# Attention and MLP in one core: more elementwise work for GpSimd, a planner that counts eight transfers, and free PSUM banks for the last layer

## The chip, the cores and the metric

The kernel runs on one core of a Trainium2 chip. The metric is the device time of one execution in microseconds (us), the median of several runs. A core has TensorE (PE, matrix multiply, written to PSUM), VectorE (DVE), ScalarE (ACT) and GpSimd (POOL) for elementwise work, and SyncE (SP), which here issues all DMA transfers. Each engine runs its own instructions in order; they wait for each other through semaphores. In the profile, PEld is the loading of weights into PE.

## The reference

Attention where a query sees only the keys of its own hash bucket, over 4 batches, 8 heads, 768 positions and 64 dimensions, and then an MLP on the 3072 resulting rows:

```python
q_bucket = np.sum((np.einsum('bhsd,dk->bhsk', q, proj) > 0) * powers, axis=-1)   # 6 bits; k likewise
mask = q_bucket[:, :, :, None] == k_bucket[:, :, None, :]
scores = np.where(mask, scale * np.matmul(q, k.transpose(0, 1, 3, 2)), -1000000000.0)
attn = softmax(scores)
x = np.matmul(attn, v)             # laid out as 3072 rows of 512
h = np.maximum(x @ w_in, 0.0)      # w_in 512 x 2048
out = (h * h) @ w_out              # w_out 2048 x 512
```

## The kernel before, in words

Float32 products are made from pairs of half-precision numbers: each operand is split into a high part and the difference that the high part leaves, and three products (high by high, high by low, low by high) are summed in PSUM. Splitting is a copy (`move`, lines 465 to 471) and a subtraction (`left`, lines 473 to 477; for the weights the lines 579 and 580 in `split`). Much of the elementwise work is this.

**Attention** goes in units of 128 queries of one head (`unit`, line 739), 192 in all, six to a visit: one visit is a pair of heads and half of the positions (384 rows). A unit's scores are gathered by four matmuls in `pS`, two PSUM banks (for some early ones `pS2`, in the banks of `po`); DVE moves them out to `e` and takes the extreme value; ACT takes the exponential; the reciprocal of the sum, `rv`, is made on GpSimd or DVE; then `hl`, the high part (ACT) and the difference (DVE, since its scale is a vector), and a transposing DMA into `aT`. In the first four visits (`PLAIN_AV`) GpSimd multiplies `e` by `rv` instead and PE transposes it (`pT`), out of which ACT moves it to `aT`. `av` (line 783) multiplies with the values into `pA`, one bank, and leaves `xx`, again in two parts. `prep` (line 631) makes ready what a head needs: `A` and `L` are the two parts of the input `R`, `M` and `Q` carry the mask of the buckets, moved about by small DMAs. `first` (line 664) does it for the first visit with fewer steps, and uses `codes`.

**The MLP** (`moe`, line 807) has eight layers of 384 rows (a batch and a half each), and may run as soon as the four visits of its rows are done. Of its 16 steps f, each takes twelve `pm` matmuls, then relu (`g32`), the square (`square`, line 561), the high part `g[:, 0]` and the difference `g[:, 1]`; and a step later nine `po` matmuls, three for each of three groups t of 128 rows. The tile `po` has three banks, one for each group. After the last step the three groups are moved out to `o` and sent. There is one `pm` and one `po`, and two buffers of `g` and `g32`. The weights are fetched and split (`fetch`, `split`) during the first visits and the first layer, and `verify` reads all inputs again and checks that they lie in the range for which this fast way holds; the second half of the last layer's steps waits for its answer.

**The order** is made by a planner at build time. The code above doesn't issue instructions; it adds operations to a `Program`, some with several possible engines ("ways"). `add` (line 169) works out dependencies from the regions that operations touch (`region`, line 156); `order` simulates all five queues forward and backward several times and keeps the shortest plan; `emit` issues the instructions of each queue in the order of the plan. So whatever the planner believes of the chip sets which engine an operation gets and its place in the queue; the waits themselves are made afterwards, by the tile framework. Its beliefs are:

- `cost` (line 195): nanoseconds of each operation.
- `PRICE` (line 42): in the choice of an engine (lines 365 to 372) the operation's time is multiplied by it, and what else is ready for that engine is added.
- `port` (line 235): which operations hold something that DVE and GpSimd share; `forward` does not start one while another holds it (lines 361 to 363, 374 to 376).
- `region`: for PSUM, the banks an access touches, where two reads of one bank are ordered too (line 184).
- the transfers: how long SP is taken by issuing one, and when it lands (lines 384 to 391).

`LOW_BY` (line 63) names the engines that may take the differences of the weight splits.

## Time and profile before

| | |
|---|---|
| median of three runs | 832.88 us (832.54 to 834.76) |
| the profiled execution | 834.86 us, its span 833.1 us |
| granted TensorE clock, mean over the span | 0.994 |
| bytes moved by DMA | 145.93 MB, of which 56.80 MB read from HBM and 6.29 MB written |
| instructions | 14383 |

The span runs from the first to the last instruction; the time of the execution also holds what lies around it. All comparisons of busy time, idle time and waits are against the span. In a view of the profile, a row such as "PE x <- ACT y: 5.7, 8, 0.9" says that PE stood idle for 5.7 us in all, 8 times, 0.9 us at the longest, in front of an operation that writes x, until ACT's operation on y ended. A row of the timeline gives the start, the length, the engine, the line, the operation, out<-in with partitions x elements, how often it ran in a row, and in square brackets the idle time before it with what ended it. Nearly all operations have line 427, where the planner's helper issues them, so they are told apart by tile and shape.

### The profile page before, as it was taken

To read this page: it belongs to the slowest core of one execution; us is meant where nothing else is said; L and a number is where in the kernel's file an instruction comes from. 1 tells how busy PE (TensorE), PEld (TensorE's weight loads), DVE (VectorE), ACT (ScalarE), POOL (GpSimd) and SP (SyncE) were. 2 spreads that over 40 slices of the span, in tenths; PEclk is the share of its full clock that TensorE was granted. 3 is DMA by queue.
4 is the path that set the end of the run, shared out by engine and by line. 5 is a ranking of instruction groups with operands and counts; after the bars stand their busy time and mean duration, and the time that the engine had idled before them with its cause. 6 is when DMAs were issued, how large, how long until landed. Compare 5 with 4: busy or idle time off the path is not lost. (4 is left out here: it accounts for less than half of the span.)

```text
span 833.1 us, 14383 instructions
## 1 busy us (share of the span) xinstructions
PE 794.3 (95%) x5001; PEld 430.0 (52%) x5001; DVE 605.2 (73%) x1200; ACT 656.6 (79%) x1238; POOL 72.7 (9%) x175
## 2 busy tenths in 40 slices
PE   7797799999999999999999999999999999999996
PEld 4354355555555554555555545555555554555553
DVE  6888989998999888898879755888889433611110
ACT  5898999998888989888898856888988997334443
POOL 1255200100000010000000000000002000000000
PEclk9999999999999999999999999999999999999999
DMA  8985979999999999999989866988975889501001
GB/s 258 270 223 181 292 188 179 214 176 195 183 202 196 195 188 213 192 181 219 194 188 186 212 165 140 181 143 148 146 133 99 239 290 304 212 1 39 1 1 42
DMA packets 299521, 145.93 MB, mean 175 GB/s; under 512 B 268752, under 2 KB 279344, under 8 KB 299440
## 3 DMA queue, kind: packets, MB, share of 16 engines
q1 hardware_dynamic: 299440, 144.93, 77.2%
q8 instruction: 41, 0.67, 0.3%
q14 instruction: 40, 0.33, 0.1%
HBM read 56.80 MB, written 6.29 MB: 76 GB/s over the span
## 5 line engine op out<-in xcount | busy, mean ns | idle before, releaser
L427 PE MATMUL po<-wo,g 128*128 128x512 f16 x1152 | 296.9, 379 | 5.7 <-ACT o L427 5.7
L427 PE MATMUL pm<-xx,win 128*128 128x384 f16 x1536 | 297.7, 326 | 4.4 <-ACT g L427 2.8
L427 PEld LDWEIGHTS <-win 128*128 128x128 f16 x1536 | 149.9, 98 | 116.6 <-issue 8.0
L427 DVE TENSOR_SCALAR_CACHE_REDUCE e<-pS 128x768 f32<-128x768 f32 x192 | 182.7, 953 | 21.9 <-PE pS L427 17.7
L427 ACT ACTIVATE e<-e,maxes 128x768 f32<-128x768 f32 x192 | 178.2, 929 | 20.7 <-DVE e L427 19.2
L427 DVE SCALAR_TENSOR_TENSOR hl<-e,rv,hl 128x768 f16<-128x768 f32 x168 | 171.0, 1019 | 18.8 <-ACT hl L427 17.8
L427 PEld LDWEIGHTS <-g 128*128 128x128 f16 x1152 | 111.9, 98 | 124.8 <-issue 9.1
L427 ACT ACTIVATE hl<-e,rv 128x768 f16<-128x768 f32 x168 | 154.6, 923 | 6.0 <-DMA aT<-hl 5.2
L427 DVE SCALAR_TENSOR_TENSOR g<-g,g 128x384 f16<-128x384 f32 x121 | 66.9, 553 | 111.8 <-ACT g L427 111.4
L427 ACT ACTIVATE g<-g 128x384 f32<-128x384 f32 (+1 forms) x251 | 129.4, 517 | 6.6 <-PE po L427 2.7
L427 ACT ACTIVATE g<-pm 128x384 f32<-128x384 f32 x127 | 61.2, 482 | 90.3 <-PE pm L427 90.0
L427 PE MATMUL pS<-A,Q 128*128 128x384 f16 x372 | 93.1, 330 | 4.1 <-DVE e L427 2.6
L427 PE MATMUL pS<-L,M 128*128 128x384 f16 x372 | 91.8, 327 | 0.8 <-DMA M<-Q 0.8
L424 PE MATMUL pA<-aT,VV 128*64 128x384 f16 x1008 | 87.2, 327 | 0.0
L427 POOL TENSOR_SCALAR rv<-sums 128x1 f32<-128x1 f32 x136 | 36.8, 271 | 541.7 <-ACT e L427 400.2
L424 PEld LDWEIGHTS <-VV 128*64 128x64 f16 x1008 | 54.7, 110 | 32.9 <-issue 10.0
L427 PEld LDWEIGHTS <-Q 128*128 128x128 f16 x372 | 34.2, 98 | 43.1 <-issue 16.2
L427 DVE TENSOR_SCALAR M<-pc,masks 128x384 f16<-128x384 f32 x64 | 43.0, 672 | 15.4 <-PE pc L427 15.2
L427 PEld LDWEIGHTS <-M 128*128 128x128 f16 x372 | 36.3, 98 | 25.1 <-DMA M<-Q 1.2
L427 ACT ACTIVATION_READ_ACCUMULATOR e<-e,maxes 128x1 f32 x192 | 36.6, 191 | 0.0
L427 DVE SCALAR_TENSOR_TENSOR L<-R,A 128x768 f16<-128x768 f32 x32 | 30.4, 950 | 7.7 <-ACT A L427 7.5
L427 PE MATMUL pT<-unit_f,e 128*128 128x128 f32 x144 | 23.8, 293 | 10.5 <-ACT aT L427 7.7
(82 smaller groups left out, 517.4 us busy)
## 6 DMA issues: line engine op xcount, KB each, us to landing
R<-kq SPq DMA_DIRECT2D x32, 384.0 KB, 3.8
X<-kq SPq DMA_DIRECT2D x32, 384.0 KB, 4.1
raw<-w_in SPq DMA_DIRECT2D x16, 511.8 KB, 5.6
raw<-w_out SPq DMA_DIRECT2D x16, 511.8 KB, 4.9
V<-vp SPq DMA_DIRECT2D x20, 384.0 KB, 5.1
out<-o SPq DMA_DIRECT2D x24, 256.0 KB, 2.7
X<-vp SPq DMA_DIRECT2D x16, 384.0 KB, 4.4
Q<-L SPq DMA_DIRECT2D x32, 96.0 KB, 2.9
```

The lines of the kernel that those rows point to most:

```text
L424: ins = q.engine.matmul(*map(real, args), **kw).ins
L427: ins = getattr(q.engine, o.name)(*map(real, o.args), **{k: real(x) for k, x in o.kw.items()}).ins
```

## The change

The planner gets other beliefs, and the MLP other PSUM tiles at its end:

- `PRICE`: ACT 0.3 becomes 1, GpSimd 3.06 becomes 1.5.
- `port`: a DVE operation with two tensor inputs in SBUF no longer counts as a holder of what is shared with GpSimd; only copies and `tensor_scalar` do.
- `region`: an access to a PSUM tile counts as one to the whole tile, and two reads of it are no longer ordered.
- `cost`: pairs of matmuls with 64 rows of weights are counted as partly beside each other.
- `LANES`: the planner holds SP back where eight transfers are under way.
- `codes` shares its buffer with `g32`.
- in the last layer the three groups are gathered in the two banks of `pS` and the bank of `pA`, which attention no longer needs, instead of in `po`.
- the move of group t = 1 out of PSUM goes to DVE; that of the others may still go to ACT or DVE.

```diff
-PRICE = dict(pe=1, dve=3.57, act=0.3, pool=3.06, sp=0.43)
+PRICE = dict(pe=1, dve=3.57, act=1, pool=1.5, sp=0.43)
...
+LANES = 8
...
         if rec.kind == "psum":
-            return 0, 1, f0 // 512, 1 + (f0 % rec.row + size(ap.ap[1:]) - 1) // 512, 0, 0, 0
+            return 0, 1, 0, 1, 0, 0, 0
...
-                if (w or w2 or rec.kind == "psum") and a0 < p1 and p0 < a1 and b0 < f1 and f0 < b1 and not (fs and fs == bs and (c1 <= g0 or g1 <= c0)):
+                if (w or w2) and a0 < p1 and p0 < a1 and b0 < f1 and f0 < b1 and not (fs and fs == bs and (c1 <= g0 or g1 <= c0)):
...
             t = sum(size(a[2]) * column.get(a[2].dtype, 1 / 2.4) + 7 for a, _ in args) / side
+            if args[0][0][1].shape[0] == D and len(args) == 2:
+                t *= 0.5 if args[0][0][2].dtype == F32 else 0.7
             return t, t
...
-        return inside and (len(ins) == 2 or name in ("tensor_copy", "tensor_scalar"))
+        return inside and name in ("tensor_copy", "tensor_scalar")
...
                 dma += done
                 done = dma + 910 - t
+                if k != "pool":
+                    lanes.append(t + done)
+                    if len(lanes) >= LANES:
+                        busy = max(busy, lanes[-LANES] + 60 - t)
...
-        codes = sb([P, 4 * P], BF16, "codes")
+        codes = sb([P, 4 * P], BF16, "codes", 2, tag="g32")
...
                 if first:
-                    po = ps([P, 3, DM], F32, "po")
+                    if fast and n == 2 * B - 1:
+                        po = ps([P, 2, 512], F32, "pS"), ps([P, 512], F32, "pA")
+                        po = [po[0][:, 0], po[0][:, 1], po[1]]
+                    else:
+                        po = ps([P, 3, DM], F32, "po")
+                        po = [po[:, t] for t in range(3)]
...
                     elif last:
                         o = sb([P, DM], F32, "o", tag="f")
-                        move(o, po[:, t], back)
+                        move(o, po[t], back, (dve,) if fast and t == 1 else (act, dve, pool))
                         send(out[r0 : r0 + P], o)
```

More of the change, by code (lines that the diff above doesn't have):

```diff
@@ L326, in forward @@
         free = dict.fromkeys(keys, 0.0)
-        out, dma, dge, held, kind = [], 0.0, 0.0, 0.0, None
+        out, dma, dge, held, kind, lanes = [], 0.0, 0.0, 0.0, None, []
         def offer(i):
@@ L848, in moe @@
                     pr.rank, pr.mark = RANK_PE, pace()
-                    pe.matmul(po[:, t], gh, wo[:, 0, m], start=first, stop=False)
-                    pe.matmul(po[:, t], gh, wo[:, 1, m], start=False, stop=False)
-                    pe.matmul(po[:, t], gl, wo[:, 0, m], start=False, stop=last)
+                    pe.matmul(po[t], gh, wo[:, 0, m], start=first, stop=False)
+                    pe.matmul(po[t], gh, wo[:, 1, m], start=False, stop=False)
+                    pe.matmul(po[t], gl, wo[:, 0, m], start=False, stop=last)
                     pr.mark = None
@@ L861, in moe @@
                         if m == 3:
-                            move(acc[:, t], po[:, t], back)
+                            move(acc[:, t], po[t], back)
                         else:
-                            dve.scalar_tensor_tensor(acc[:, t], po[:, t], back, acc[:, t], ALU.mult, ALU.add)
+                            dve.scalar_tensor_tensor(acc[:, t], po[t], back, acc[:, t], ALU.mult, ALU.add)
                         if m == NF - 1:
```

## The prediction, made before the changed kernel was run

> **What bounds the kernel now.** I read the page's first two parts first: the busy shares and the 40 slices.
>
> ```profile
> span 833.1 us, 14383 instructions
> PE 794.3 (95%) x5001; PEld 430.0 (52%) x5001; DVE 605.2 (73%) x1200; ACT 656.6 (79%) x1238; POOL 72.7 (9%) x175
> PE   7797799999999999999999999999999999999996
> ...
> DVE  6888989998999888898879755888889433611110
> ACT  5898999998888989888898856888988997334443
> ...
> PEclk9999999999999999999999999999999999999999
> ```
>
> TensorE (PE) is nearly full from slice 6 on, at a granted clock of 0.9 or more throughout. Its idle time is 833.1 - 794.3 = 38.8 us, and only that can be won. The view of busy time by stretch says where it lies:
>
> ```profile
> 0.00:104.00 104.00, 80.78 (x523) 46.38 (x524) 85.51 (x189) 86.63 (x173) 36.56 (x54) 0.97 0.83 245
> 104.00:650.00 546.00, 540.50 (x3523) 293.46 (x3522) 470.95 (x925) 471.35 (x859) 36.18 (x121) 1.00 0.90 179
> 650.00:720.00 70.00, 68.10 (x399) 35.55 (x398) 28.65 (x52) 54.14 (x122) 0.00 (x0) 1.00 0.91 286
> 720.00:833.00 113.00, 104.93 (x562) 54.60 (x560) 20.07 (x37) 44.46 (x87) 0.00 (x0) 0.98 0.07 26
> ```
>
> After length come busy PE, PEld, DVE, ACT, POOL. PE idles 23.2 us in the front (first attention units, no MLP work yet), 5.5 us in the long middle, 1.9 and 8.1 us later. So off-loading DVE and ACT in the middle wins at most 5.5 us: there PE, not they, sets the time. After 720 us DVE and ACT are mostly idle already. The waits of PE name what it lacked:
>
> ```profile
> PE pT L427 <- ACT aT L427: 7.7, 8, 2.2
> PE po L427 <- ACT o L427: 5.7, 8, 0.9
> PE pc L427 <- ACT bits L427: 3.0, 2, 2.8
> ...
> PE pT L427 <- POOL e L427: 2.5, 3, 1.1
> ...
> PE pS L427 <- DMA A<-A: 1.3, 1, 1.3
> PE pS L427 <- DMA M<-Q: 0.8, 1, 0.8
> ```
>
> The second row is what the change can reach most surely. The timeline of the end shows its form:
>
> ```profile
> 822.75 1.46 PE L427 MATMUL po<-wo,g 128*128 128x512 f16 x6
> ...
> 824.25 0.60 ACT L427 ACTIVATE o<-po 128x512 f32<-128x512 f32 x1 [1.64 <-PE po L427]
> ...
> 824.90 0.81 PE L427 MATMUL po<-wo,g 128*128 128x512 f16 x3 [0.69 <-ACT o L427]
> ...
> 825.74 0.60 ACT L427 ACTIVATE o<-po 128x512 f32<-128x512 f32 x1 [0.90 <-PE po L427]
> 826.39 0.59 PE L427 MATMUL po<-wo,g 128*128 128x512 f16 x2 [0.69 <-ACT o L427]
> ```
>
> The three matmul groups of one `po` tile lie in three banks, yet the second waits until the first has been moved out, and the third for the second: 0.69 us each. The wait is on the tile, not on the bank, while the planner's `region` of before counts banks and so puts the move ahead of the next group.
>
> **The change part by part.** First a piece of the chain of waits, for a length that is needed at once:
>
> ```profile
> 752.32 1.95 PE pm L427 x12
> ```
>
> *The whole PSUM tile as one region, the DVE move for t=1, free banks for the last layer.* With whole tiles, a move depends on all groups written before it in program order, so the three groups run together and then the three moves. The 8 stalls, 5.7 us, go; what is late next is the following layer's first `po` group, which must wait for the moves: about 2 x 0.60 on ACT beside one on DVE. Twelve `pm` matmuls, 1.95 us, lie between and cover it; without that cover it costs 7 handovers x 1.2 = 8.4 us. The last layer doesn't wait even then, its banks (`pS`, `pA`) being free. Bounds -5.7 and +2.7 (8.4 - 5.7); I take **-5**, near the rows that show the stalls. Eight moves of t=1 go to DVE, behind whatever DVE runs at that moment; that is hidden by the same `pm`. The read-against-read orders that go away concern only moves on two engines; no row of PE's waits names one, so 0.
>
> *GpSimd's share.* I read "a third" as a third of 192 differences (128 `g`, 32 `L`, 32 weight splits) and of 144 squares. The prices:
>
> ```profile
> L427 POOL TENSOR_SCALAR e<-e,rv 128x768 f32<-128x768 f32 x24 | 24.5, 1028 | 14.9 <-PE pT L427 6.1 <-DVE rv L427 5.9 <-ACT aT L427 2.2
> L427 POOL TENSOR_TENSOR g<-g,g 128x384 f16<-128x384 f32 x7 | 6.5, 933 | 15.1 <-ACT g L427 9.8 <-DVE rv L427 3.1 <-issue 2.1
> L427 POOL TENSOR_TENSOR win<-f,win 128x512 f16<-128x512 f32 x3 | 3.5, 1173 | 4.1 <-ACT win L427 4.0
> ```
>
> ```profile
> L427 DVE SCALAR_TENSOR_TENSOR hl<-e,rv,hl 128x768 f16<-128x768 f32 x166 | 168.9, 1019 | 18.7 <-ACT hl L427 17.8
> ...
> L427 DVE SCALAR_TENSOR_TENSOR g<-g,g 128x384 f16<-128x384 f32 x79 | 43.4, 550 | 6.3 <-ACT g L427 6.0
> ...
> L427 DVE SCALAR_TENSOR_TENSOR L<-R,A 128x768 f16<-128x768 f32 x24 | 22.8, 951 | 3.6 <-ACT A L427 3.4
> ```
>
> ```profile
> L427 ACT ACTIVATE g<-g 128x384 f32<-128x384 f32 x86 | 44.4, 517 | 1.1
> ```
>
> The DVE rows and the ACT row are those of the middle alone. A GpSimd square and a GpSimd `L` aren't in the trace. The square lies between DVE's 0.55 and 1.17 (more columns); I take 0.93, the same two-input form. `L` lies between 1.03 (one input) and 1.87 (twice 0.93); I take 1.87. In the middle about 20 more `g` differences, 30 squares, 8 `L` and 3 splits move: 20 x 0.93 + 30 x 0.93 + 8 x 1.87 + 3 x 1.17 = 65 us onto GpSimd. DVE loses 20 x 0.55 + 8 x 0.95 + 3 x 0.68 (split, 0.68 in the timeline below) = 20.6 us, ACT 30 x 0.517 = 15.5 us. As PE is full, none of it counts directly.
>
> What counts is what the moved work does to DVE. Two places in the trace show a GpSimd operation beside a DVE operation with two SBUF inputs:
>
> ```profile
> 639.80 0.92 POOL L427 TENSOR_TENSOR g<-g,g 128x384 f16<-128x384 f32 x1 [2.70 <-ACT g L427]
> 639.83 1.71 DVE L427 SCALAR_TENSOR_TENSOR hl<-e,rv,hl 128x768 f16<-128x768 f32 x1
> ...
> 647.06 1.00 DVE L427 SCALAR_TENSOR_TENSOR hl<-e,rv,hl 128x768 f16<-128x768 f32 x1
> ```
>
> ```profile
> 19.12 0.69 DVE L427 TENSOR_TENSOR win<-f,win 128x512 f16<-128x512 f32 x1
> ...
> 80.00 2.73 POOL L427 TENSOR_SCALAR e<-e,rv 128x768 f32<-128x768 f32 x2
> 80.04 1.92 DVE L427 TENSOR_TENSOR win<-f,win 128x512 f16<-128x512 f32 x2 [0.34 <-ACT win L427]
> ...
> 82.89 0.48 PE L427 MATMUL pS<-A,Q 128*128 128x384 f16 x2 [1.39 <-DVE e L427]
> ```
>
> `hl` took 1.71 instead of 1.00 us; two splits took 1.92 instead of 2 x 0.69, two `e` 2.73 instead of 2.06, and PE then stood 1.39 us for DVE. So each meeting costs about 0.71 us, and the new `port` tells the planner that it costs nothing. In the middle, `hl`, `g` and `L` alone are 168.9 + 43.4 + 22.8 = 235 of 546 us of DVE, 43%; 61 moved operations x 0.43 x 0.71 = 18.6 us of blocking, about what DVE was relieved of. DVE therefore stays near 471 of 546 us, with some 75 us of slack, but the slack is no longer where the plan has it. Between none and all reaches PE: 0 and +18.6. I take **+2**, one in ten, since the seven `g` on GpSimd today stand in a middle with 5.5 us of PE idle time in all.
>
> The Trainium skill, page "SBUF — State Buffer", section "SBUF: two separate sides", says that GpSimd and a DVE operation with two SBUF inputs lock a shared port for whole instructions, the later one blocking fully. By that, the 0.89 us of overlap at 639.83 would cost 0.89 (the trace has 0.71) and the blocking 61 x 0.43 x 0.89 = 23.3 us; it speaks against the new `port`.
>
> *The front.* It begins and ends with these:
>
> ```profile
> 6.78 1.55 PE L424 MATMUL pS<-K,G 64*128 64x384 f32 x4
> ...
> 97.70 0.32 PE L427 MATMUL pm<-xx,win 128*128 128x384 f16 x1 [1.04 <-ACT xx L427]
> ```
>
> About 3 `L` and 4 splits leave DVE: 3 x 0.95 + 4 x 0.69 = 5.6 us of 85.5; meetings give back 7 x 0.43 x 0.71 = 2.1. ACT, as busy (86.6), gets relief where the price 1 in place of 0.3 sends copies elsewhere. GpSimd has 104 - 36.6 = 67 us free, but its `e` (24 x 1.03) sit on each unit's path to `pT`, and a 1.17 or 1.87 us piece ahead of one delays it. Bounds: the front's idle time without the 6.8 us until the first data matmul, 23.2 - 6.8 = -16.4, and +7.2 (four units each behind a 1.8 us piece). I take **-2**, about half of what DVE sheds.
>
> *Eight transfers under way.* Nothing on the chip changes by it but SP's order. The stalls it counts exist in the front:
>
> ```profile
> SPq L427 <- DMA raw<-w_out: 6.6, 6, 1.7
> SPq L427 <- DMA L<-M: 6.0, 3, 4.6
> ```
>
> PE itself waited for transfers only 1.3 + 0.8 = 2.1 us (rows above), so it is worth -2.1 to +2.1; I take 0. The factor for 64-row matmuls concerns the first visit's scores, `codes` in a `g32` buffer is read long before `g32` is written: 0.
>
> **Sum:** -5 + 2 - 2 = -5 us. The profiled execution took 834.86 us (span 833.1, 1.8 around it); it becomes 829.9. The median of before, 832.88, is 2.0 lower, so the forecast is **827.9**.
>
> **The rivals.**
>
> *GpSimd blocks DVE on the path (slower).* The place is the middle: DVE's `e` out of `pS` comes late, and PE, in order, stands as at 82.89. On top of 18.6 us of blocked DVE, a GpSimd square or difference that starts behind `hl` waits for half of 1.02, 61 x 0.43 x 0.51 = 13.4 us, on the way to `po`. For it: the rows above, and a planner blind to it. Against: DVE's 75 us of slack, MLP matmuls that fill PE. It decides once 7 + 2.5 = 9.5 of these 32 us, 30%, reach PE. At 60%: -7 + 19 = +12, **845**. By the skill's lock, with 0.89, it is +15. Chance 0.26.
>
> *Nothing comes of it.* The handover stalls become waits for the moves (ACT is 86% busy in the middle, so a move queues), front and blocking cancel: -1, **832**. Chance 0.17.
>
> *The front opens.* ACT and DVE both shed a tenth of the front's 86 us, and the MLP starts 8 us earlier: -5 + 2 - 8 = -11, **822**. For it: GpSimd idle there. Against: PE waits there mostly for ACT's `aT` and `bits`, which GpSimd can't take. Chance 0.13.
>
> *The planner keeps GpSimd idle*, because ready queues on ACT and DVE stay short: only the handovers, -5, with no blocking, **828**, as forecast. Chance 0.05.
>
> **How the numbers follow.** The forecast has 0.39. This kernel's measurement can tell about 0.3%, 2.5 us, from no change. Faster: 0.35 of the forecast's 0.39, the front's 0.13, the idle GpSimd's 0.05 and 0.02 of "nothing comes of it": 0.55. Same: the forecast's other 0.04 and 0.14 of "nothing": 0.18. Slower: 0.26 and the last 0.01: 0.27. The terms' bounds span -24 to +31 us; cutting 0.1 at each end gives 816 to 845. The forecast's own range is 823 to 831.
>
> **What would show it.** Right: no `po` wait on `o`; the last two moves on two engines; GpSimd near 150 to 200 us busy; DVE's busy time about as before, with `hl` above 1.02 us; PE idle in the middle still near 5 us. Wrong: PE waits on DVE `e` or GpSimd `g` above 10 us in the middle (the blocking), `po` waits that stay, or a first `pm` well before or after 97.7 us (the front). The first falls if GpSimd's `g` is much longer than 0.93 us.

## The result, and the profile after

The changed kernel takes **845.26 us** (median of four runs, 842.59 to 848.99); the kernel before, beside it, 833.63 (832.54 to 834.76). The ratio is 1.0154, its 95% interval 1.0118 to 1.0189. The forecast was 827.9 with a range of 816 to 845: a change forecast to win 5 us costs 11.6, and the time lies just above the range. The profiled execution took 846.62 us, 11.8 more than that of before.

First the page of the changed kernel, the busy shares and the slices:

```profile
span 844.8 us, 14501 instructions
PE 805.8 (95%) x5014; PEld 436.0 (52%) x5014; DVE 548.5 (65%) x1053; ACT 615.3 (73%) x1143; POOL 338.3 (40%) x417
PE   8787779999999999999999999999999999999996
...
DVE  4788779878888788878888603787889241045000
ACT  3788888897888878888888755777786468763342
POOL 2699875344243543333344332343222222331221
PEclk9899899999999999999999999999999999999999
```

The relief came: DVE is 57 us less busy (605.2 to 548.5), ACT 41 (656.6 to 615.3). But GpSimd (POOL) went from 72.7 to 338.3 us, not to the 150 to 200 of the prediction, and it is nearly full in slices 3 to 5, where the row of before has the digits 5, 5 and 2:

```profile
POOL 1255200100000010000000000000002000000000
```

PE stands idle as long as before, 844.8 - 805.8 = 39.0 us against 38.8, and is 11.5 us busier with the same arithmetic. So the idle time of PE, on which the prediction was built, doesn't show the loss. One reason is in the last row: in slices 2 and 5 the granted clock is below 0.9, and a slow matmul counts as busy.

The view of busy time by stretch, with the stretches of before (after length: PE, PEld, DVE, ACT, POOL, granted clock), has all of it in the first row:

```profile
0.00:104.00 104.00, 81.37 (x471) 47.40 (x472) 76.38 (x163) 76.76 (x148) 75.26 (x80) 0.90 0.82 246
...
104.00:650.00 546.00, 538.03 (x3488) 291.09 (x3487) 429.31 (x812) 430.71 (x775) 214.74 (x280) 1.00 0.88 174
...
650.00:720.00 70.00, 68.78 (x410) 36.13 (x408) 22.17 (x50) 47.77 (x96) 16.74 (x19) 1.00 0.60 145
...
720.00:844.00 124.00, 117.64 (x651) 61.41 (x648) 20.67 (x30) 60.10 (x126) 31.59 (x39) 0.99 0.37 123
```

In the first 104 us PE is as busy as before (81.37 against 80.78) but runs 471 matmuls instead of 523, at a granted clock of 0.90 instead of 0.97.

To have one number for this I worked out PE's **lost time**: each matmul is given the spacing that its form has in an unbroken run at full clock (`pm` and scores 0.163 us, `po` 0.216, and so on; the `idle` matmuls that only fill gaps, zero), and the lost time at t is t minus the spacings of all matmuls begun by then. The arithmetic is 776.1 us in both kernels. Lost time, in us:

| by | 20 | 60 | 97 | 130 | 650 | last matmul |
|---|---|---|---|---|---|---|
| before | 12.8 | 22.2 | 33.8 | 36.1 | 45.4 | 50.5 |
| after | 15.6 | 30.8 | 42.0 | 52.3 | 59.3 | 61.1 |

By 130 us the changed kernel has lost 52.3 - 36.1 = **16.2 us more**; from there to the end it loses 8.8 instead of 14.4, **5.6 less**. The last matmul begins 10.7 us later, and the end comes another 1 us later. Such a count is of the one profiled execution of a kernel, while its time is a median; the two lie up to 3 us apart (here 846.62 and 845.26, before 834.86 and 832.88).

The loss belongs to the front, the gain to the handovers. One more of PE's waits before, beside those that the prediction shows:

```profile
PE pS L427 <- DVE e L427: 2.6, 4, 1.4
```

And after:

```profile
PE pT L434 <- POOL e L434: 8.2, 7, 2.3
PE pS L434 <- DVE e L434: 6.9, 14, 1.2
...
PE pT L434 <- ACT aT L434: 2.9, 4, 2.0
...
PE po L434 <- POOL g L434: 1.5, 3, 0.8
...
PE po L434 <- ACT o L434: 0.6, 1, 0.6
```

These waits of PE show both. `po` on `o` fell from 5.7 to 0.6 us. `pT` on GpSimd's `e`, which exists only in the first four visits, rose from 2.5 to 8.2, and `pS` on DVE's `e` from 2.6 to 6.9. But `pT` on ACT's `aT` fell from 7.7 to 2.9, so the waits also moved from ACT to GpSimd and DVE: in the first 130 us PE's idle time grew by 4.4 us in all (23.8 to 28.2), about a quarter of the 16.2.

What GpSimd does in the front is in the groups of the first 98 us. Before, DVE alone:

```profile
L427 DVE SCALAR_TENSOR_TENSOR f<-raw,top 128x512 uint32<-128x512 uint32 x22 | 15.3, 698 | 0.9 <-ACT top L427 0.9
...
L427 DVE TENSOR_TENSOR win<-f,win 128x512 f16<-128x512 f32 x10 | 7.8, 785 | 1.5 <-ACT win L427 1.5
L427 DVE SCALAR_TENSOR_TENSOR L<-R,A 128x768 f16<-128x768 f32 x8 | 7.6, 950 | 4.1 <-ACT A L427 4.1
L427 DVE TENSOR_TENSOR wo<-f,wo 128x512 f16<-128x512 f32 x7 | 4.8, 679 | 0.0
```

After, GpSimd:

```profile
L434 POOL TENSOR_SCALAR e<-e,rv 128x768 f32<-128x768 f32 x22 | 26.7, 1222 | 5.1 <-DVE rv L434 5.0
L434 POOL TENSOR_TENSOR win<-f,win 128x512 f16<-128x512 f32 x10 | 12.3, 1233 | 12.1 <-ACT win L434 11.8
L434 POOL TENSOR_TENSOR L<-R,A 128x768 f16<-128x768 f32 x6 | 9.9, 1645 | 0.0
L434 POOL TENSOR_TENSOR wo<-f,wo 128x512 f16<-128x512 f32 x6 | 7.9, 1312 | 2.1 <-ACT wo L434 1.8
L434 POOL TENSOR_SCALAR win<-f 128x512 f16<-128x512 f32 x6 | 4.4, 735 | 2.9 <-DVE f L434 2.6
...
L434 POOL TENSOR_SCALAR wo<-f 128x512 f16<-128x512 f32 x5 | 3.8, 756 | 0.9 <-DVE f L434 0.6
```

And DVE:

```profile
L434 DVE SCALAR_TENSOR_TENSOR f<-raw,top 128x512 uint32<-128x512 uint32 x22 | 20.7, 939 | 3.2 <-ACT top L434 3.2
...
L434 DVE TENSOR_TENSOR win<-f,win 128x512 f16<-128x512 f32 x4 | 4.6, 1157 | 1.6 <-POOL win L434 1.3 <-ACT win L434 0.3
L434 DVE SCALAR_TENSOR_TENSOR L<-R,A 128x768 f16<-128x768 f32 x2 | 3.5, 1746 | 1.2 <-ACT A L434 1.2
...
L434 DVE TENSOR_TENSOR wo<-f,wo 128x512 f16<-128x512 f32 x2 | 1.5, 750 | 0.5 <-POOL wo L434 0.5
```

GpSimd took 6 of 8 `L`, 16 of the weights' differences and 11 of their high parts. What stayed on DVE grew longer each time: `f`, the same 22 operations, from 698 to 939 ns, `L` from 950 to 1746, `win` from 785 to 1157. Worse, GpSimd's `e` stands in one queue with all this. Two timelines show one case of each mechanism; first the collision:

```profile
18.23 1.65 POOL L434 TENSOR_TENSOR L<-R,A 128x768 f16<-128x768 f32 x1
18.30 2.12 DVE L434 TENSOR_TENSOR win<-f,win 128x512 f16<-128x512 f32 x1 [0.74 <-POOL win L434]
...
20.35 0.94 DVE L434 TENSOR_SCALAR_CACHE_REDUCE e<-pS 128x768 f32<-128x768 f32 x1
...
21.35 0.91 PE L431 MATMUL pS<-K,G 64*128 64x384 f32 x2 [1.07 <-DVE e L434]
```

A difference that takes 0.69 us alone took 2.12 behind GpSimd's `L`; DVE's move of the scores came late, and PE stood 1.07 us. Then the queue, in GpSimd's own timeline:

```profile
46.36 2.22 POOL L434 TENSOR_SCALAR e<-e,rv 128x768 f32<-128x768 f32 x2 [0.32 <-DVE rv L434]
48.55 1.65 POOL L434 TENSOR_TENSOR L<-R,A 128x768 f16<-128x768 f32 x1
50.16 1.60 POOL L434 TENSOR_TENSOR win<-f,win 128x512 f16<-128x512 f32 x1
51.85 0.19 POOL L434 TENSOR_SCALAR rv<-sums 128x1 f32<-128x1 f32 x1
52.13 0.62 POOL L434 TENSOR_SCALAR win<-f 128x512 f16<-128x512 f32 x1
52.83 1.47 POOL L434 TENSOR_TENSOR win<-f,win 128x512 f16<-128x512 f32 x1
54.29 0.90 POOL L434 TENSOR_SCALAR e<-e,rv 128x768 f32<-128x768 f32 x1
```

Between one unit's `e` and the next there are 5.7 us of other work almost without a gap. In the timeline of all engines the second `e` could have begun at 52.57 us, when DVE had made its reciprocal; it waited 1.7 us behind the two pieces of `win`, and PE's `pT` 0.39 us for it. The first `pm`, which waits for the `xx` at the end of the first attention, came at 112.26 instead of 97.70 us:

```profile
112.26 0.32 PE L434 MATMUL pm<-xx,win 128*128 128x384 f16 x1 [0.23 <-ACT xx L434]
```

At the other end, the kernel's last matmuls and moves:

```profile
836.60 0.60 ACT L434 ACTIVATE o<-pS 128x512 f32<-128x512 f32 x1 [2.22 <-PE pS L434]
837.23 2.04 SPq L434 DMA_DIRECT2D out<-o  x3
837.23 0.69 DVE L434 TENSOR_SCALAR o<-pS 128x512 f32<-128x512 f32 x1 [58.51 <-ACT o L434]
837.68 0.60 ACT L434 ACTIVATE o<-pA 128x512 f32<-128x512 f32 x1 [0.48 <-PE pA L434]
```

The groups no longer wait for the moves. But DVE's move, of another bank of the same tile, began only when ACT's had ended, and the row names ACT's `o` as what it waited for. The stretch from the last matmul's end to the span's end grew from 833.1 - 826.98 = 6.1 to 844.8 - 837.64 = 7.2 us. The transfers, now issued in a row, explain little of that: the last one was issued at 838.93 and landed 2.9 us later, 4.2 us after the last matmul; before, it was issued at 827.64 and landed 3.3 us later, 4.0 us after it. What fills the rest isn't known.

### The profile page after: what moved, and what is told of

It is laid out like the page before. It is cut to its first block, busy times and chain, and to the rows that moved or that the text cites. A ratio compares the mean times of both kernels' runs of the same rounds, so it can differ in the third digit from the quotient of the medians.

```text
span 844.8 us, 14501 instructions
## 1 busy us (share of the span) xinstructions
PE 805.8 (95%) x5014; PEld 436.0 (52%) x5014; DVE 548.5 (65%) x1053; ACT 615.3 (73%) x1143; POOL 338.3 (40%) x417
## 4 chain that ended last, share of the span: by engine, by line
PE 73%; ACT 7%; issue 6%; DVE 6%; POOL 4%; DMA 3%; ACTq 0%; POOLq 0%; DVEq 0%
PE pm L434 24%; PE po L434 21%; PE pS L434 13%; PE pA L431 8%; ACT e L434 2%; DVE e L434 2%; DMA aT<-hl 1%; DVE hl L434 1%; ACT hl L434 1%; PE pA L434 1%; PE pd L431 1%; ACT g L434 1%; PE pS L431 1%; PE pc L434 1%; PE pT L434 1%
## 5 line engine op out<-in xcount | busy, mean ns | idle before, releaser
L434 PE MATMUL pm<-xx,win 128*128 128x384 f16 x1536 | 309.3, 326 | 2.1 <-ACT g L434 1.6
L434 PE MATMUL po<-wo,g 128*128 128x512 f16 x1008 | 279.1, 379 | 2.3 <-POOL g L434 1.5
L434 ACT ACTIVATE e<-e,maxes 128x768 f32<-128x768 f32 x192 | 178.7, 931 | 58.3 <-DVE e L434 55.8
L434 DVE TENSOR_SCALAR_CACHE_REDUCE e<-pS 128x768 f32<-128x768 f32 x192 | 182.4, 952 | 54.3 <-PE pS L434 49.8
L434 DVE SCALAR_TENSOR_TENSOR hl<-e,rv,hl 128x768 f16<-128x768 f32 x168 | 187.9, 1120 | 36.9 <-ACT hl L434 34.8
L434 PEld LDWEIGHTS <-win 128*128 128x128 f16 x1536 | 149.8, 98 | 115.1 <-issue 6.6
L434 POOL TENSOR_TENSOR g<-g,g 128x384 f16<-128x384 f32 x122 | 116.4, 954 | 189.4 <-ACT g L434 144.6
L434 PEld LDWEIGHTS <-g 128*128 128x128 f16 x1152 | 111.4, 98 | 124.2 <-issue 6.8
L434 ACT ACTIVATE hl<-e,rv 128x768 f16<-128x768 f32 x148 | 136.9, 926 | 10.3 <-DMA aT<-hl 5.6
L434 ACT ACTIVATE g<-pm 128x384 f32<-128x384 f32 x128 | 62.0, 484 | 96.2 <-PE pm L434 94.4
L434 ACT ACTIVATE g<-g 128x384 f32<-128x384 f32 (+1 forms) x204 | 106.1, 521 | 10.1 <-PE po L434 5.4
L434 PE MATMUL pS<-A,Q 128*128 128x384 f16 x372 | 94.9, 330 | 7.1 <-DVE e L434 6.9
L434 PE MATMUL pS<-L,M 128*128 128x384 f16 x372 | 94.4, 331 | 0.0
L434 POOL TENSOR_SCALAR rv<-sums 128x1 f32<-128x1 f32 x116 | 39.4, 340 | 136.5 <-ACT e L434 104.7
L434 POOL TENSOR_TENSOR L<-R,A 128x768 f16<-128x768 f32 x30 | 51.1, 1707 | 30.3 <-ACT A L434 29.9
L434 POOL TENSOR_SCALAR g<-g 128x384 f16<-128x384 f32 x51 | 28.6, 562 | 84.2 <-ACT g L434 73.8
L434 DVE TENSOR_SCALAR M<-pc,masks 128x384 f16<-128x384 f32 x64 | 42.9, 671 | 27.6 <-PE pc L434 27.5
L434 PEld LDWEIGHTS <-Q 128*128 128x128 f16 x372 | 35.6, 99 | 43.6 <-issue 15.7
L434 PEld LDWEIGHTS <-M 128*128 128x128 f16 x372 | 36.8, 99 | 25.1 <-issue 1.8
L434 PE MATMUL pT<-unit_f,e 128*128 128x128 f32 x144 | 26.9, 324 | 13.0 <-POOL e L434 8.2
```

The source lines that it names most:

```text
L434: ins = getattr(q.engine, o.name)(*map(real, o.args), **{k: real(x) for k, x in o.kw.items()}).ins
```

## The experiments

The traces left three candidates: the front's volume on GpSimd (queueing and collisions), the planner that no longer sees collisions (`port`), and the count of transfers. The planner makes a further difficulty. It finds its order by search, so any edit also draws another order, and a difference of a few us may be luck. Some runs therefore change nothing but the prices by 1%. The two prices of the change, ACT's and GpSimd's, were not run apart, and neither the factor for 64-row matmuls nor the shared buffer of `codes` was run alone. All kernels compute the whole of the reference. "Lost" is as above, by 130 us and after it.

### Old prices, old rule, no count, splits off GpSimd

The changed kernel with one belief or part undone in each.

The old prices:

```diff
-PRICE = dict(pe=1, dve=3.57, act=1, pool=1.5, sp=0.43)
+PRICE = dict(pe=1, dve=3.57, act=0.3, pool=3.06, sp=0.43)
```

> The changed kernel with the old prices (ACT 0.3, GpSimd 3.06), everything else as changed. Theory 1, GpSimd's queue in the front (it was busy 75 of the first 104 us and its e, which PE transposes, waited in it): GpSimd falls back to about 75 us busy, the first pm comes near 98 us instead of 112.3, and the time is about 14 us less than the changed kernel's 845, near 831, a little under before because the handover gain stays. Theory 2, the order of the first transfers (eight under way): nothing much changes, first pm still near 110 us, time 842 or more. Theory 3, the plan that no longer knows that DVE and GpSimd block each other: GpSimd has little work left to block with, so as theory 1, but DVE's hl should go back to 1.02 us.

Measured 832.85 us, ratio 0.9998 [0.9984, 1.0013]; GpSimd busy 82.1 us. Without the new prices GpSimd gets little work, and neither loss nor gain is left.

The old rule:

```diff
-        return inside and name in ("tensor_copy", "tensor_scalar")
+        return inside and (len(ins) == 2 or name in ("tensor_copy", "tensor_scalar"))
```

> The changed kernel with the old port rule (a DVE operation with two SBUF inputs holds what is shared), new prices kept. Theory 1: the prices put the work on GpSimd, so GpSimd stays above 250 us busy and the first pm stays later than 105 us; time 838 to 846. Theory 3: the plan now reckons with the blocking, hl goes back below 1.05 us, the first pm comes near 100 us, time 833 or less. Theory 2: first pm near 110 us whatever the rule.

Measured 836.86, 1.0057 [1.0037, 1.0076], between the times of the theories 1 and 3. The surprise is what stayed: GpSimd is busy 326.1 us in all and 77.1 in the first 104, about as much as in the changed kernel (338.3 and 75.3), and `f` takes 890 ns in both, over the whole kernel. Yet PE's wait for GpSimd's `e` is 2.8 us instead of 8.2, and 41.7 us are lost by 130 us instead of 52.3.

No count of transfers:

```diff
-LANES = 8
+LANES = 10000
```

> The changed kernel without the count of eight transfers under way. Theory 2: the first scores and the sgn_f transfers go back to their old places (codes ready near 8.6 us, first e out of pS near 13.8 instead of 16.0 us), and the front gets 3 to 5 us shorter or more; time near 838. Theories 1 and 3: GpSimd as busy as in the changed kernel (over 300 us), first pm later than 108 us, time 842 to 848.

Measured 849.28, 1.0202 [1.0177, 1.0227]. The count isn't what costs; without it the kernel is no faster.

The splits off GpSimd:

```diff
-TOP_BY, LOW_BY = ("dve", "act"), ("dve", "pool")
+TOP_BY, LOW_BY = ("dve", "act"), ("dve",)
...
-                move(hi, f)
+                move(hi, f, 1.0, (act, dve))
```

> The changed kernel with the weight splits (both the half-precision copy and the difference) kept off GpSimd; prices, port rule and all else as changed. Theory 1: in the front GpSimd loses about 37 of its 75 us, its e no longer queues, the wait of PE's pT for GpSimd's e falls from 8.2 to under 4 us, and the first pm comes 8 to 14 us earlier than 112.3; time 831 to 838, although GpSimd keeps its g work in the middle. Theory 3 with its place in the middle (hl blocked by g): hl stays near 1.12 us and the time near 843.

Measured 840.79, 1.0099 [1.0076, 1.0122], worse than expected. GpSimd's share of the first 104 us fell from 75.3 to 55.4 us and the time lost by 130 us from 52.3 to 40.9, eleven of the sixteen us; but after 130 us this plan lost 15.2 us where the changed kernel lost 8.8. Half of the front's gain was given back later.

### Both beliefs old, another order, `e` on DVE, and the handover alone

First the old prices and the old rule together, each by its line above.

> The changed kernel with both old prices and the old port rule: what is left of the change are whole PSUM tiles, the DVE move, the free banks, eight transfers, the factor and the shared buffer. With it stands a square of four kernels: new price and new rule 845.3, new price and old rule 836.9, old price and new rule 832.9. Theory 1 (GpSimd's load in the front, made by the price): the rule counts only where the price loads GpSimd, so this one lies within 2 us of 832.9. Theory 3 (the rule by itself misleads the plan): some 4 to 8 us below 832.9.

Measured 832.81, 1.0001 [0.9985, 1.0018]. With the old prices the rule doesn't matter (832.85 with the new one). This kernel has the new handover too, yet it is no faster than before; whether the factor or the shared buffer takes back what the handover gives (below), or the order does, isn't known.

The changed kernel in another order:

```diff
-PRICE = dict(pe=1, dve=3.57, act=1, pool=1.5, sp=0.43)
+PRICE = dict(pe=1, dve=3.6, act=1, pool=1.51, sp=0.43)
```

> The changed kernel with DVE's price 3.60 for 3.57 and GpSimd's 1.51 for 1.50: a shift of under 1% that no theory gives a meaning, but the planner makes another order of it. It tells how far a plan's accident goes. If the result of the change is a cause and not an accident: 840 to 850 and a first pm of 107 to 115 us. If it was an accident of one order: anything down to 833.

Measured 845.03, 1.0155 [1.0127, 1.0183], lost by 130 us 48.7. The loss isn't the bad luck of one order.

`e` on DVE in the first four visits:

```diff
-DIVIDE = (0, 1, 2, 3), ("pool",)
+DIVIDE = (0, 1, 2, 3), ("dve",)
```

> The changed kernel with the 24 products e times rv of the first four visits on DVE instead of GpSimd; prices and rule as changed. Theory 1: what delays the front is that e waits in GpSimd's queue and on what is shared; GpSimd loses about 29 of its 75 us there, PE's wait of pT for e (8.2 us) falls to under 3, and the first pm comes 6 us or more before 112.3; time 833 to 840. Rival: the front is bound by the sum of elementwise work on DVE and ACT; DVE then gets 13 us more and the first pm stays at 110 us or later, time 843 or more.

Measured 844.60, 1.0148 [1.0121, 1.0176]: the time that the rival gave (843 or more), though the first `pm` came at 105.5 us and not at 110 or later. Its waits of PE:

```profile
PE pS L434 <- DVE e L434: 7.1, 17, 1.4
PE pT L434 <- DVE e L434: 4.3, 4, 3.1
```

The wait moved with `e`: DVE, 88.2 us busy in the first 104, makes PE wait where GpSimd had. 45.4 us are lost by 130 us, 6.9 less than in the changed kernel, and 15.6 after it, 6.8 more. So GpSimd's queue ahead of `e` isn't the sole cause. That fits a front that is short of both engines.

The kernel before, with the handover alone:

```diff
-            return 0, 1, f0 // 512, 1 + (f0 % rec.row + size(ap.ap[1:]) - 1) // 512, 0, 0, 0
+            return 0, 1, 0, 1, 0, 0, 0
...
-                if (w or w2 or rec.kind == "psum") and a0 < p1
+                if (w or w2) and a0 < p1
```

`po`, the free banks and DVE's move are as in the change; all else is as before.

> The kernel before with only whole PSUM tiles as regions, the DVE move for group 1 and the free banks of the last layer. The prediction's term: PE's 5.7 us of waits for o go and the time falls by 4 to 6 us, to about 828. Rival (the handover's end isn't what ends the kernel: PE waits elsewhere instead): the po waits go, but the time stays within 2 us of before.

Measured **829.67**, 0.9969 [0.9950, 0.9987]: faster than both kernels, and the best version found. Its waits of PE:

```profile
PE po L427 <- ACT o L427: 0.5, 1, 0.5
```

The stall is gone as in the changed kernel, and after 130 us this kernel loses 9.6 us instead of 14.4. The time fell by 2.7 us (832.34 beside it), less than the 4 to 6 expected. The profiled execution, 826.88 us, was the fastest of its ten.

### Dose: only `g` on GpSimd, only the front on GpSimd, and two controls

Only `g` (and, in the units, `rv`, `e` and `hl`) on GpSimd: the splits off it by the two lines above, and `prep`'s work too, where `False` says that GpSimd isn't to have it:

```diff
-            move(A, R, balance)
-            left(L, R, balance, f32(A))
+            move(A, R, balance, (act, dve))
+            left(L, R, balance, f32(A), False)
...
-        move(VV[:, :, :, 0:D], RV, vscales[b][0])
+        move(VV[:, :, :, 0:D], RV, vscales[b][0], (act, dve))
```

> The changed kernel, new prices and new rule, but GpSimd may no longer take the weight splits, A, L or VV: what it keeps is e and rv, the g work of the MLP and some hl. Front theory: the loss is made before the first pm by the pieces of work that GpSimd gets there, and its g work in the middle is harmless; GpSimd still has over 230 us busy and hl stays near 1.1 us, but the first pm comes at 93 to 99 us and the time is 827 to 833. Middle theory (the prediction's slower rival: DVE blocked in the middle): 838 or more, whatever the first pm.

Measured 833.94, 1.0029 [1.0013, 1.0046], just above the 827 to 833 of the front theory. Here GpSimd still does 245.7 us of work, 127 of the 128 `g` differences among it, and the planner is still blind to collisions. `hl` takes 1076 ns on average (before 1019), `f` 746; 38.6 us are lost by 130 us and 9.5 after it. Of the 16.2 us lost in the front 13.7 are gone, and by the ratios (1.0154, 1.0029) four fifths of the loss.

The handover alone, and the front's work on GpSimd, where `True` says that only GpSimd may have it:

```diff
-TOP_BY, LOW_BY = ("dve", "act"), ("dve", "pool")
+TOP_BY, LOW_BY = ("dve", "act"), ("pool",)
...
-            left(L, R, balance, f32(A))
+            left(L, R, balance, f32(A), fast and b == 0)
```

> The kernel before with whole PSUM tiles and free banks (829.7, first pm at 92.9 us), old prices and old rule, but with all 32 differences of the weight splits and the eight L of the first batch made on GpSimd; nothing is added to GpSimd in the middle or at the end. Front theory: this alone brings most of the loss: the first pm comes 5 to 12 us later and the time is 835 to 842; DVE's f gets longer than 0.8 us (0.70 before). Middle theory: first pm within 2 us of 92.9, time near 830.

Measured 833.51, 1.0019 [1.0000, 1.0038], 3.8 us above the handover alone, with the old prices and the old rule. That is less than expected (835 to 842), and `f` takes 791 ns, just under the 0.8 us named. This is roughly the front's share by itself: all 32 differences of the weights and the first 8 `L`. Its row for the first 104 us, and GpSimd's:

```profile
0.00:104.00 104.00, 78.20 (x502) 42.89 (x503) 69.26 (x164) 86.43 (x172) 70.45 (x76) 0.98 0.85 246
```

```profile
L427 POOL TENSOR_TENSOR win<-f,win 128x512 f16<-128x512 f32 x13 | 16.3, 1260 | 3.4 <-ACT win L427 3.4
L427 POOL TENSOR_TENSOR L<-R,A 128x768 f16<-128x768 f32 x8 | 13.1, 1645 | 9.4 <-ACT A L427 9.3
```

Against the handover alone, GpSimd has 26 us more here (70.45 against 44.25) and DVE 17 less (69.26 against 86.53), as the change wants it, and yet 502 matmuls are begun instead of 539, 41.7 us are lost by 130 us instead of 33.8, and the first `pm` comes at 105.0 instead of 92.9 us. Relieving DVE in the front by way of GpSimd costs time there even when the planner sees the collisions (here it had no choice of engine).

The kernel before in another order:

```diff
-PRICE = dict(pe=1, dve=3.57, act=0.3, pool=3.06, sp=0.43)
+PRICE = dict(pe=1, dve=3.6, act=0.3, pool=3.08, sp=0.43)
```

> The kernel before with DVE's price 3.60 for 3.57 and GpSimd's 3.08 for 3.06: another order of the same work, for the scatter that a new plan brings by itself. If plans of the same beliefs agree: 830 to 835, first pm 95 to 100 us. If the scatter is larger than that, differences of 3 us between the other kernels mean nothing.

Measured 832.02, 1.0009 [0.9987, 1.0030]: the same time.

The handover alone, and the count:

```diff
+LANES = 8
...
+                if k != "pool":
+                    lanes.append(t + done)
+                    if len(lanes) >= LANES:
+                        busy = max(busy, lanes[-LANES] + 60 - t)
```

> The kernel before with whole PSUM tiles, free banks and the count of eight transfers. If the count is worth what it seemed worth in the changed kernel (849.3 without it, 845.3 with it), 826 or less and a first pm at or before 92.9 us. If that was the scatter of plans, 829 to 834.

Measured 829.96, 0.9982 [0.9963, 1.0000], against 829.67 without: the count is worth nothing that can be measured here.

### Where the rule acts

The old rule in the front alone, that is, for DVE's operations other than `hl` and `g`; then in the middle alone, for these two; then the whole old rule on the kernel with only `g` on GpSimd:

```diff
-        return inside and name in ("tensor_copy", "tensor_scalar")
+        return inside and (len(ins) == 2 and args[0].rec.name not in ("hl", "g") or name in ("tensor_copy", "tensor_scalar"))
...
-        return inside and name in ("tensor_copy", "tensor_scalar")
+        return inside and (len(ins) == 2 and args[0].rec.name in ("hl", "g") or name in ("tensor_copy", "tensor_scalar"))
```

> The changed kernel (new prices) where the old port rule holds for DVE's two-input operations except hl and g: the planner reckons with the blocking of f, L, VV and the weight splits, nearly all of which run in the front, and not with that of hl and g in the middle. If the rule's 8.4 us (845.3 with the new, 836.9 with the old) are lost in the front: 834 to 840, with TensorE's lost time at 130 us near the 41.7 us of the old rule and not the 52.3 of the new. If they are lost in the middle, or by the scatter of plans: 842 to 848.

> The counterpart: the changed kernel where the old port rule holds for hl and g alone. If the rule's 8.4 us are lost in the front: 842 to 848 and lost time at 130 us of 47 us or more. If in the middle: 834 to 840.

> New prices with the old port rule, GpSimd kept off weight splits, A, L and VV. If both parts of the loss lie in the front and GpSimd's g work is harmless, this is as fast as the kernel before with the MLP's new tiles (829.7), 828 to 832, with GpSimd above 200 us busy; were g on GpSimd a gain in itself it would be below 828. If the middle loses by it: 834 or more.

Measured 841.17 (1.0088 [1.0059, 1.0117]), 838.45 (1.0070 [1.0044, 1.0096]) and 841.15 (1.0087 [1.0058, 1.0117]). They don't fall in line. The rule in the front brought the loss by 130 us down to 38.1, but 18.5 came after it; the rule in the middle gave 41.6 and 10.7, better in the front than expected for a rule of the middle. And with only `g` on GpSimd the old rule made the kernel slower, 841.15 against 833.94, though by 130 us it had lost little more, 40.8 against 38.6; the difference came after, 17.4 against 9.5. Either part helps the whole change a little, neither is the whole, and the size of it is that of another draw of the order. So the question became whether the rule does anything beyond such draws.

### The rule against the draw of an order

Two price variants of 1% for the old rule, and the second of them for the new rule too:

```diff
-PRICE = dict(pe=1, dve=3.57, act=1, pool=1.5, sp=0.43)
+PRICE = dict(pe=1, dve=3.6, act=1, pool=1.51, sp=0.43)
+PRICE = dict(pe=1, dve=3.54, act=1, pool=1.49, sp=0.43)
```

> The changed kernel with DVE's price 3.54 for 3.57 and GpSimd's 1.49 for 1.50, a third order of the same beliefs after 845.3 and 845.0. If the new rule is a cause: 842 to 850 again, TensorE's lost time at 130 us 47 us or more. If those two agreed by accident: anywhere from 836 to 850.

> The changed kernel with the old port rule (836.9), DVE's price 3.60 for 3.57 and GpSimd's 1.51 for 1.50. If the rule is worth some 8 us: 834 to 840 and lost time at 130 us of 38 to 43 us. If 836.9 was one lucky order: up to 848.

> As the last, with 3.54 and 1.49. If the rule is worth some 8 us: 834 to 840 and lost time at 130 us of 38 to 43 us. If 836.9 was one lucky order: up to 848.

Measured 841.45 (1.0104 [1.0086, 1.0121]; under the 842 and the 47 us lost that were expected of a cause), 833.99 (1.0003 [0.9991, 1.0016]) and 836.64 (1.0040 [1.0025, 1.0056]). Three orders with each rule at the new prices:

| | us | mean | lost by 130 us |
|---|---|---|---|
| new rule | 845.26, 845.03, 841.45 | 843.9 | 52.3, 48.7, 44.2 |
| old rule | 836.86, 833.99, 836.64 | 835.8 | 41.7, 42.2, 39.5 |

The times don't overlap: taking collisions out of the planner's view costs about 8 us at these prices, three orders against three, and most of it before 130 us. Within each rule orders differ by 3 to 4 us, and the nearest two of different rules by 4.6. The last column is weaker than it looks, for the profiled executions of the old rule took 834.39, 836.84 and 833.70, up to 2.9 us off their medians. And it holds for this plan; with only `g` on GpSimd the one order tried of each rule stood the other way round, by 7 us.

The main runs in one table, by time. The runs of before beside the different groups of experiments have medians of 832.3 to 833.5 us, and the lost time is that of one execution, so differences of 3 us in it mean nothing by themselves:

| kernel | us | lost by 130 us | lost after 130 us | GpSimd busy, us |
|---|---|---|---|---|
| handover alone | 829.67 | 33.8 | 9.6 | 79.0 |
| before, 31 runs beside "only `g`" | 832.37 | 36.1 | 14.4 | 72.7 |
| both beliefs old | 832.81 | 35.9 | 11.3 | 79.6 |
| old prices | 832.85 | 36.4 | 12.6 | 82.1 |
| handover, front's work on GpSimd | 833.51 | 41.7 | 6.9 | 113.6 |
| only `g` on GpSimd | 833.94 | 38.6 | 9.5 | 245.7 |
| old rule | 836.86 | 41.7 | 8.6 | 326.1 |
| splits off GpSimd | 840.79 | 40.9 | 15.2 | 320.3 |
| only `g` on GpSimd, old rule | 841.15 | 40.8 | 17.4 | 232.9 |
| `e` on DVE | 844.60 | 45.4 | 15.6 | 321.5 |
| the change | 845.26 | 52.3 | 8.8 | 338.3 |
| no count | 849.28 | 50.0 | 12.5 | 343.2 |

## Why the prediction was wrong

**The step that failed is the term of the front, "-2" with the bound "+7.2".** Instead of winning 2 us, PE had lost 16.2 us more by 130 us, over twice the bound. The sizes in it failed, and by them its sign:

- *The volume.* "About 3 `L` and 4 splits leave DVE" rests on "a third", which no row gave. The planner decides, and at the new prices it moved 17 differences off DVE in the first 98 us (8, 10 and 7 operations became 2, 4 and 2) and gave GpSimd 11 high parts besides. In the whole kernel it took 122 of 128 `g` differences and 30 of 32 `L`, but one square of 128; "a third" fits neither.
- *The price of a meeting.* Those three groups became 10.6 us shorter on DVE (7.8 + 7.6 + 4.8 to 4.6 + 3.5 + 1.5), but `f` alone gave back 5.4 (15.3 to 20.7), where the term had 2.1 for all meetings. All in all 34.1 us more on GpSimd in these 98 us (36.09 to 70.18) came with 6.7 us less of DVE and 8.8 less of ACT, while PE ran 450 matmuls instead of 485.
- *The cover of `e`.* The bound allowed "four units each behind a 1.8 us piece". GpSimd had 67 us free and the planner filled nearly 40 of them; the 22 `e` took 1222 ns each instead of 1028, and PE's wait for them rose by 5.7 us. But with `e` on DVE the time was nearly the same (844.60), so this was not the loss by itself.
- *The clock.* The sum has no term for it, by "a granted clock of 0.9 or more throughout" and "only that can be won" of PE's idle time. A slice is a mean: before, too, the clock is 0.50 for two stretches of 3.4 us in the front, and after for six.

The busy times of DVE, ACT and GpSimd up to the first `pm` of before are from these rows, first that kernel, then the changed one:

```profile
0.00:97.70 97.70, 74.65 (x485) 43.33 (x485) 79.60 (x175) 80.62 (x162) 36.09 (x53) 0.97 0.83 242
```

```profile
0.00:97.70 97.70, 76.99 (x450) 45.07 (x450) 72.90 (x153) 71.79 (x139) 70.18 (x74) 0.91 0.83 250
```

What the runs show of the cause: with the old prices the loss is gone (832.85). At the new prices and the new rule, taking the front's work off GpSimd in part (the splits) or whole (only `g`) brings the time lost by 130 us down to 40.9 and 38.6, where three orders of the change have 44.2 to 52.3; giving GpSimd that work alone raises it from 33.8 to 41.7 and the time by 3.8 us. And at the new prices the blind planner costs about 8 us. The time itself follows the front less surely: 840.79 and 833.94 us in those two, and 841.15 in another order of "only `g`", with the old rule. From the handover alone, 829.7, the three orders with the old rule are 6.1 us higher (3.0 from "both beliefs old"), and those with the new rule another 8.1.

**What stays open** is how the rule acts. GpSimd's share, `f` and `hl` (1098 against 1120 ns) hardly differ between the old and the new rule, PE's wait for `e` does, but not in every order (5.5 us in the second variant of the old rule, 4.0 in the first variant of the new); and half of the rule did not put the effect in one stretch. What differs in all three orders is the share of DVE and ACT in the first 104 us: DVE is busy 76.4, 79.1 and 84.2 us with the new rule and 71.4, 73.3 and 75.6 with the old, ACT 76.8, 79.4 and 81.7 against 83.7, 83.0 and 84.6. Whether the rule costs its time by that was not tested.

The slow clock is part of the loss, but doesn't decide between the rules. At half clock a stretch of 3.4 us costs at most 1.7, so the four more of the changed kernel make at most 6.8 of the 16.2 us. The rest is the 4.4 us of idle time, 2.3 us more of `idle` matmuls by 130 us (6.2 to 8.6), and some 3 us that I put down to broken runs of matmuls. Each of the six dips, and of the two before, follows within 2.0 us a gap of PE of 1.1 to 2.8 us, so the dips look like an effect of the gaps; not every such gap has one. As to the rules: runs of the third order of the change took 841.2 to 842.6 us at a mean granted clock of 0.993 to 0.995, and one of the first variant of the old rule 834.81 at 0.985.

**The middle, "+2", held for this plan.** `hl` went from 1019 to 1120 ns:

```profile
L434 DVE SCALAR_TENSOR_TENSOR hl<-e,rv,hl 128x768 f16<-128x768 f32 x168 | 187.9, 1120 | 36.9 <-ACT hl L434 34.8 <-POOL hl L434 1.4
...
L434 POOL TENSOR_TENSOR g<-g,g 128x384 f16<-128x384 f32 x122 | 116.4, 954 | 189.4 <-ACT g L434 144.6 <-issue 30.7 <-PE po L434 5.7
```

That is 168 x 0.101 = 17 us of blocking, near the 18.6 worked out, but by luck: two errors cancel. GpSimd got 214.74 - 36.18 = 179 us more in the middle, not 65, so a meeting cost much less than supposed there. The 0.71 us were read off one meeting; the second pair of rows in the prediction gives 1.92 - 1.38 = 0.54 us for two, and in the same timeline as the first the `hl` at 644.61, 0.44 us beside a `g`, took 1.24 us, 0.24 more than alone. DVE, rid of the `g`, was busy 429 us of the middle's 546 and absorbed it: between 130 and 650 us PE lost 7.0 us, before 9.3, the handover alone about 7.2. So "DVE's busy time about as before" was wrong, in the harmless direction. More work on GpSimd isn't harmless in every plan: four of the experiments lost 15 to 18 us after 130 us, the handover alone 9.6.

**The handover, "-5", had the right mechanism and about twice the size.** Waits fell by 5.1 us; what lies after 130 us fell by 5.6. By itself it is worth 2.7 us of time, 0.9969 [0.9950, 0.9987], that is 1.1 to 4.2 us. One detail was wrong: "2 x 0.60 on ACT beside one on DVE". The moves of two banks of one tile ran one after the other (0.63 us from ACT's start to DVE's), and the stretch after the last matmul is 1.1 us longer. **The count of transfers, "0"**, held: 829.96 against 829.67.

**The rival "GpSimd blocks DVE on the path"** gave the time, 845, and a mechanism that the trace shows, DVE's `e` late behind a blocked operation. It named the wrong place, so that its number came true is luck. Its point of decision, 30% of the blocking reaching PE in the middle, was never reached; the front, where there is no MLP work beside the units, decided. The listed sign "a first `pm` well after 97.7 us" is the one that came true; "`po` waits that stay" did not, nor the waits above 10 us in the middle (4.3 us in all on DVE's `e` and GpSimd's `g`). "The front opens" named the right place with the wrong sign: its condition, a tenth less of DVE and ACT in the front, came about (85.5 to 76.4 and 86.6 to 76.8 us), and the MLP began 14.6 us later instead of 8 earlier.

**A meeting at its dearest.** At 18.30 us the difference began 0.07 us after a 1.65 us `L` and took 2.12 us instead of 0.69. The Trainium skill, page "SBUF — State Buffer", section "SBUF: two separate sides", has the later of two such operations blocked for the whole of the earlier one. By that it would take 1.58 + 0.69 = 2.27 us; the trace agrees but for 0.15 us. The two meetings of `hl` above fall short of the overlap by about as much, 0.71 of 0.89 us and 0.24 of 0.44. So in these three rows a meeting costs its overlap less 0.15 to 0.20 us, and no flat price.

## What to carry to other kernels

When a planner's prices change, count what the new prices can move, and not a share taken from a description; an engine with idle time in a stretch is not free there if its queue holds a step of the only work that the bound engine has. Read a change per stretch, and where busy time hides slow or broken runs of matmuls, count work done by a given time instead of idle time. And before a few us are explained by an edit to something that reorders everything, draw the order again: here the same kernel with prices 1% apart lay 3.8 us apart. A trace is one execution, too, and can lie 3 us from the median that it is set beside.

## What the runs showed of the hardware that wasn't expected

- GpSimd's `L` (128x768, two inputs) takes 1.65 us in the front (1.71 on average over the kernel) where the prediction took 1.87, so twice the 128x384 price overstates it.
- PE's granted clock halves (0.50) in dips of 3.4 us, in some kernels of two to four times that, all but one of them, until the last matmul, in the front, where PE has its gaps: in the profiled executions two before, six in the changed kernel, none in the kernel with the handover alone, whose longest gap there is 1.4 us (the granted clock of its first 104 us is 1.00, against 0.97 and 0.90). PE needn't stand still for long: in the 3.4 us ahead of each of the eight dips it was busy for 0.7 to 2.3 us. The one dip in the middle, in "only `g`" with the old rule at 321.9 us, follows a gap of 2.1 us. The row of the handover alone:

```profile
0.00:104.00 104.00, 83.62 (x539) 45.37 (x540) 86.53 (x191) 89.64 (x182) 44.25 (x56) 1.00 0.85 251
```

- ACT and DVE don't read two banks of one PSUM tile side by side in these kernels. The trace names ACT's move as what ended DVE's wait (`[58.51 <-ACT o L434]`), so by the trace it is the waits that order them; whether the chip could do both at once was not tried.
